# A layer norm split in two inside a streaming decode kernel, and an output written as 32 rows of 128

## The chip, the cores and the metric

The kernel runs on one core of one Trainium2 chip. The metric is device time in microseconds (us): the median of several executions. Where two kernels are compared, the ratio is the mean time of one kernel's fast runs over that of the other's fast runs of the same rounds on the same chip, so it is not quite the quotient of the medians quoted beside it. Kernels are compared only within the same rounds.

## The reference, cut to what matters

Eight tokens (batch 8, one position each) of width 512 go through attention, feed-forward, attention, feed-forward. Each part is preceded by a layer norm and added to its input. Both attentions read the same caches: 8 batches x 8 key heads x 8192 positions x 128, for K and for V.

```python
def _layernorm(x, axis=-1, eps=1e-5):
    m = jnp.mean(x, axis=axis, keepdims=True)
    v = jnp.var(x, axis=axis, keepdims=True)
    return (x - m) / jnp.sqrt(v + eps)

x = A_x
x = x + _A_ref(_layernorm(x), A_k_cache, A_v_cache, A_wq, A_wo)   # 32 query heads, 4 to a key head
x = x + _B_ref(_layernorm(x), B_w1, B_w2)                          # 512 -> 1792, silu, -> 512
x = x + _A_ref(_layernorm(x), A_k_cache, A_v_cache, A_wq, A_wo)
x = x + _B_ref(_layernorm(x), B_w1, B_w2)
return x
```

## The kernel before

The caches of one batch are used for the first and at once for the second attention of that token, so they are read from memory once. Where token b changes from its first to its second attention, a short serial chain has to run: end of attention (called x2 here), norm, feed-forward, norm, queries, scores. I call such a place a crossing; there are eight, about 135 us apart. In the views below, `kts` is a slot that holds loaded keys (a K load, 2 MB), `ring` the cells that hold values (a V load, 0.5 or 1 MB), `sc` the scores, `ot` the products with the values (V matmuls) and `qtb` the queries of the second attention; a slot or a cell can be loaded again when the work that reads it is over.

The program is built by a small planner. Every piece of work is a node with an engine, an assumed duration, a priority and a list of nodes that must be over; the planner simulates the engines and so fixes the order of the instructions on each of them. Each engine is given its instructions in that order; the traces below show it keep to it (at the third crossing of the changed kernel a cast whose matmuls had ended at 391.15 starts at 397.68, after the instruction ahead of it has waited 7.16 us). Resources (`res("misc")` is one bank of PSUM) are tracked by name, and a semaphore wait follows from who last wrote or read a name.

```python
def norm_nodes(tag, prio, b0, nb, deps):
    at = 40 if nb == 1 else 472
    nm, st, sq = (MI[:, at + 8 * k:at + 8 * k + nb] for k in range(3))      # columns of the bank "misc"
    # ... cut: stats() = 8 small matmuls (minus the mean, the mean), squares() = 6 more, scaled() on ACT
    def vari():
        op(dve, lambda: dve.tensor_scalar(var[:, 0:1], nm, st, sq, op0=ALU.mult, op1=ALU.add), ...)
    def root():
        op(pool, lambda: pool.tensor_tensor(rstd[:, 0:nb], var[:, 0:nb], expo[:, 0:nb], ALU.pow),   # GpSimd
           reads=[res("var"), res("expo")], writes=[res("rstd")])
    def apply():
        op(dve, lambda: dve.tensor_scalar(
            xn[:, b0, :], xs[:, b0, :], nm, rstd[:, 0:1], op0=ALU.add, op1=ALU.mult), ...)
    # ... cut
    v = plan.add(f"{tag}.var", "DVE", 0.3 if nb == 1 else 0.6, vari, prio, [a])
    r = plan.add(f"{tag}.root", "POOL", 0.65 if nb == 1 else 1.6, root, prio, [v])
    return plan.add(f"{tag}.xn", "DVE", 0.3, apply, prio, [r])
```

The queries of the second attention come in three pieces (head groups 0, 1, and 2 with 3). All pieces go through the same columns of the bank "misc", so the matmuls of a piece wait until the cast of the piece before has read its result:

```python
    for g0, g1 in ((0, 1), (1, 2), (2, 4)):
        # ...
        pr = prio + 2 * (g0 > 0)
        m = plan.add(f"{tag}.q{g0}", "PE", 0.5 * (g1 - g0), mul, pr, wq0_n + deps + last)
        last = [plan.add(f"{tag}.qc{g0}", "DVE", 0.17, lambda ...: query_copy(...), pr, [m])]
```

And the softmax needs a maximum over partitions:

```python
    n1 = plan.add(f"mx{u}", "DVE", 0.6, mx, pr - 1, sn + [...])        # maximum of a partition's scores
    n2 = plan.add(f"ma{u}", "POOL", 0.45, mall, pr, [n1])              # partition_all_reduce on GpSimd
    n3 = plan.add(f"own{u}", "DVE", 0.17, own_max, pr - 1, [n2])       # waits for it
    n4 = plan.add(f"exp{u}", "ACT", 0.42, exp, pr, [n3] + ...)
```

## Time and profile before

| kernel before | value | from |
|---|---|---|
| time | 1140.11 us (1139.96 to 1141.31, 3 runs) | executions |
| span of the profiled run | 1143.2 us | page |
| stream of the caches | from 3 to 1127 us, 408 GB/s | windows |
| after the stream | 16.2 us | windows |
| GpSimd busy | 116.9 us, 10% of the span | page |

The table is read like this: one resource, the transfers, is busy all the time (DMA share 1.01 while the stream runs); everything else counts only where it makes the transfers stop, and after they have ended. The lines for it are in the prediction below.

### The profile page before, as it was taken

The numbers are of one execution on the slowest core, as the hardware profiler recorded it, in microseconds if no ns is written. First come the engines' busy times: TensorE is split into PE (matmuls) and PEld (weight loads), VectorE is DVE, ScalarE is ACT, GpSimd is POOL, SyncE is SP. The second block draws the span as 40 slices with busy tenths as digits, with TensorE's granted clock in tenths as the row PEclk, the third lists the DMA queues.
The fourth block names the chain that finished last, engine by engine and source line by source line (L and its number), as shares of the span: only waits on it lengthen the run. The fifth ranks groups of instructions, "written<-read, shape, count | busy, mean of one in ns | idle before, by whom it ended". The sixth has DMA issues, their size and how long they took to land.

```text
span 1143.2 us, 32166 instructions
## 1 busy us (share of the span) xinstructions
PE 715.6 (63%) x13836; PEld 395.4 (35%) x13836; DVE 605.6 (53%) x1750; ACT 153.5 (13%) x509; POOL 116.9 (10%) x295
## 2 busy tenths in 40 slices
PE   2545566675565765657565676567566576565885
PEld 1322333343332433334233333334233243232554
DVE  5753556626565356634566345662656526673331
ACT  0010111112111211111111111111111112111110
POOL 1000011101110001100111001100111101110110
PEclk9665686657667677656667567765777757776675
DMA  9999999999999999999999999999999999999994
GB/s 368 421 418 399 366 409 420 408 383 408 424 419 406 404 416 422 423 400 413 404 408 422 373 413 417 422 414 397 405 414 420 388 409 421 419 423 404 364 408 181
DMA packets 78926, 458.76 MB, mean 401 GB/s; under 512 B 8112, under 2 KB 14016, under 8 KB 51136
## 3 DMA queue, kind: packets, MB, share of 16 engines
q1 hardware_dynamic: 78784, 456.70, 98.4%
q8 instruction: 109, 1.79, 0.6%
q14 instruction: 33, 0.27, 0.1%
HBM read 456.66 MB, written 0.01 MB: 399 GB/s over the span
## 4 chain that ended last, share of the span: by engine, by line
DMA 67%; PE 19%; DVE 6%; issue 5%; ACT 2%; SPq 1%; POOL 1%; POOLq 0%; DVEq 0%; ACTq 0%
DMA ring<-in_A_v_cache_dram 53%; DMA ring<-in_A_wo_dram 9%; PE sc L897 8%; PE ot L1023 7%; DVE kts L842 3%; DMA kts<-in_A_k_cache_dram 2%; DMA kts<-in_A_v_cache_dram 2%; DMA w<-in_B_w_dram 2%; PE misc L724 1%; PE yt L1097 1%; PE ex L1045 1%; ACT ring L755 1%; SPq L414 1%; PE sc L929 1%; DVE part L1037 1%
## 5 line engine op out<-in xcount | busy, mean ns | idle before, releaser
L1023 PE MATMUL ot<-ring,p 128*8 128x256 bf16 x3904 | 243.2, 375 | 186.2 <-DMA ring<-in_A_v_cache_dram 178.1
L842 DVE STREAM_TRANSPOSE kts<-kts 128x1024 uint32<-128x1024 uint32 x256 | 308.0, 1223 | 27.6 <-DMA kts<-in_A_k_cache_dram 27.2
L897 PE MATMUL sc<-kts,bd 128*32 128x256 bf16 x4096 | 283.0, 406 | 34.3 <-DVE kts L842 19.7
L1023 PEld LDWEIGHTS ot<-ring,p 128*8 128x8 bf16 x3904 | 86.6, 97 | 262.0 <-DMA ring<-in_A_v_cache_dram 222.5
L897 PEld LDWEIGHTS sc<-kts,bd 128*32 128x32 bf16 x4096 | 116.4, 117 | 108.5 <-DVE bd L880 25.8
L923 ACT ACTIVATE p<-sc,small 128x256 bf16<-128x256 f32 x128 | 60.7, 474 | 412.2 <-DVE small L918 258.1
L914 POOL PARTITION_ALL_REDUCE small<-small x128 | 47.6, 372 | 617.8 <-DVE small L910 526.1
L1037 DVE TENSOR_TENSOR part<-ot,p 128x256 bf16<-128x256 f32 x128 | 53.1, 415 | 105.6 <-ACT p L1033 69.3
L1033 ACT ACTIVATE p<-ot 128x256 bf16<-128x256 f32 x128 | 48.9, 382 | 419.5 <-PE ot L1023 415.6
L929 PE MATMUL sc<-p,ident 128*32 128x256 bf16 x512 | 43.0, 323 | 84.1 <-ACT p L923 83.4
L880 DVE TENSOR_TENSOR bd<-sc,mask 128x64 bf16<-128x64 f32 x128 | 27.7, 216 | 104.4 <-PE sc L897 99.0
L943 POOL PARTITION_ALL_REDUCE small<-small x128 | 55.2, 431 | 228.4 <-DVE small L939 228.4
L909 DVE TENSOR_REDUCE small<-sc 128x1 f32<-128x256 f32 x128 | 53.3, 416 | 34.5 <-PE sc L897 34.4
L936 DVE STREAM_TRANSPOSE p<-sc 128x256 bf16<-128x256 bf16 x128 | 56.7, 443 | 12.8 <-PE sc L929 11.1
L929 PEld LDWEIGHTS sc<-p,ident 128*32 128x32 bf16 x512 | 15.4, 109 | 112.1 <-ACT p L923 110.4
L1045 PE MATMUL ex<-diag,p 128*128 128x4 bf16 x256 | 25.9, 171 | 36.0 <-DVE part L1037 21.5
L1097 PE MATMUL yt<-z,ring 128*128 128x4 bf16 x1024 | 36.8, 166 | 16.0 <-DMA ring<-in_A_wo_dram 15.4
L1097 PEld LDWEIGHTS yt<-z,ring 128*128 128x128 bf16 x1024 | 31.4, 102 | 39.7 <-DMA ring<-in_A_wo_dram 27.3
L1045 PEld LDWEIGHTS ex<-diag,p 128*128 128x128 bf16 x256 | 16.6, 104 | 80.7 <-ACT p L1033 49.2
L939 DVE TENSOR_SCALAR small<-hm,small 128x4 f32<-128x4 f32 x128 | 27.0, 211 | 31.3 <-ACT p L923 31.1
L918 DVE SCALAR_TENSOR_TENSOR small<-small,hm 128x4 f32<-128x4 f32 x128 | 19.2, 150 | 41.1 <-POOL small L914 40.9
L1074 DVE TENSOR_TENSOR z<-ex,rc 128x16 bf16<-128x16 f32 x64 | 10.5, 163 | 50.4 <-PE ex L1067 50.3
(96 smaller groups left out, 536.1 us busy)
## 6 DMA issues: line engine op xcount, KB each, us to landing
ring<-in_A_v_cache_dram SPq DMA_DIRECT2D x146, 1024.0 KB, 12.5
kts<-in_A_k_cache_dram SPq DMA_DIRECT2D x64, 2048.0 KB, 12.0
ring<-in_A_v_cache_dram SPq DMA_DIRECT2D x196, 512.0 KB, 7.8
ring<-in_A_wo_dram SPq DMA_DIRECT2D x64, 512.0 KB, 11.7
ring<-in_A_wq_dram SPq DMA_DIRECT2D x20, 512.0 KB, 12.6
kts<-in_A_v_cache_dram SPq DMA_DIRECT2D x5, 2048.0 KB, 20.9
kts<-in_A_wo_dram SPq DMA_DIRECT2D x2, 2048.0 KB, 14.9
w<-in_B_w_dram SPq DMA_DIRECT2D x2, 1792.0 KB, 14.9
```

Of the source, the lines that this page charges most:

```text
L842: op(dve, lambda: dve.transpose(v, v), reads=[], writes=[res("kt", g)], add=(q > 0))
L897: steps.append(lambda t=t, y=y, w=w: pe.matmul(sc[32 * t:32 * t + 32, 0:256], w, kv[:, 2 * t + y, q], start=(q == 0 and y == 0), stop=(q = ...
L909: op(dve, lambda: dve.tensor_reduce(mxr[si], sv, AX.X, ALU.max), reads=[res(*scr)], writes=[res("mxr", si)])
L923: op(act, lambda: act.activation(pt[:, :], sv, ACT.Exp, bias=bias[si], scale=SM_SCALE, accum_out=rsum[si]), reads=[res(*scr), res("bias", ...
L929: steps = [lambda P=P: pe.matmul(sc[32 * P:32 * P + 32, 256:512], src[:, P], pt[:, :], start=True, stop=True) for P in range(4)]
L936: op(dve, lambda: dve.transpose(pt[:, :], src), reads=[res(*scr)], writes=[res("p", sm)])
L943: op(pool, lambda: pool.partition_all_reduce(ssa[si], ssm[si], 128, bass.bass_isa.ReduceOp.add), reads=[res("mxp", si)], writes=[res("mxa" ...
L1023: steps.append(lambda t=t, c=c, k=k: pe.matmul(ot[32 * t:32 * t + 2 * R, 0:2 * DH], pt[:, k:k + 2 * R], vt[:, c, t], start=(P == 0 and c = ...
L1033: op(act, lambda: act.activation(pt[:, :], ot[:, 0:2 * DH], ACT.Copy), reads=[res("ot", o)], writes=[res("p", sm)])
L1037: op(dve, lambda: dve.tensor_tensor(part[:, :], ot[:, 0:2 * DH], pt[:, :], ALU.subtract), reads=[res("ot", o), res("p", sm)], writes=[res( ...
L1045: steps.append(lambda k=k, src=src, y=y: pe.matmul(EX[:, 0:R], src[:, y * DH:y * DH + DH], diag[:, R * y:R * y + R], start=(k == 0 and y = ...
L1097: steps.append(lambda j=j, dt=dt: pe.matmul(YT[:, dt * R:(dt + 1) * R], w[:, j, dt * 128:(dt + 1) * 128], zt[:, R * j:R * j + R], start=(g ...
```

## The change

The intent is to take the root of the variance off the chain. In place of (x - mean) x root ahead of the matmuls, only x - mean goes on; the products are linear, so the root can scale later steps: the tanh and the residual in the feed-forward, and the own maximum and the exponential in the second attention. Constants (4 and 128) are folded into the variance so that one root also brings the 0.5 of the silu and the scale of the softmax. The later query pieces also get a lower priority, and the output leaves as 32 rows of 128 by one matmul in place of 8 rows of 512 by four. The core of the diff:

```diff
+    def center_nodes(tag, prio, b, c, root_out, root_res, deps):
+        bs = slice(b, b + 1)
+        nm = YT[:, 16:17]
+        st, sq, steps = squares_of(bs, 1, 40, c)          # columns of the bank "misc"
+        def center():
+            op(dve, lambda: dve.tensor_scalar(xn[:, b, :], xs[:, b, :], nm, None, op0=ALU.add),
+               reads=[res("xs"), res("yt")], writes=[res("xn")])
+        def squares():
+            mms(steps, reads=[res("cst"), res("xs"), res("xd")], writes=[res("misc")])
+        def vari():
+            op(dve, lambda: dve.tensor_scalar(var[:, 0:1], nm, st, sq, op0=ALU.mult, op1=ALU.add),
+               reads=[res("misc"), res("yt")], writes=[res("var")])
+        def root():
+            op(pool, lambda: pool.tensor_tensor(root_out, var[:, 0:1], expo[:, 0:1], ALU.pow),
+               reads=[res("var"), res("expo")], writes=[root_res])
+        ... (cut)
+        v = plan.add(f"{tag}.var", "DVE", 0.3, vari, prio, [a, xc])
+        return xc, plan.add(f"{tag}.root", "POOL", 0.65, root, prio, [v])
 ... (cut)
-            op(act, lambda: act.activation(th, hp, ACT.Tanh, scale=0.5),
+            op(act, lambda: act.activation(th, hp, ACT.Tanh, scale=half),        # half = rstd for one token
 ... (cut)
-            pr = prio + 2 * (g0 > 0)
+            pr = prio if g0 == 0 or nb > 1 else count[0] - 3.5
 ... (cut)
-                mxp[si], mxa[si], -SM_SCALE, hm[:, :], op0=ALU.mult, op1=ALU.mult, accum_out=bias[si]),
+                mxp[si], mxa[si], sm_scale, hmm[:, :], op0=ALU.mult, op1=ALU.mult, accum_out=bias[si]),
-            op(act, lambda: act.activation(pt[:, :], sv, ACT.Exp, bias=bias[si], scale=SM_SCALE, accum_out=rsum[si]),
+            op(act, lambda: act.activation(pt[:, :], sv, ACT.Exp, bias=bias[si], scale=sm_scale, accum_out=rsum[si]),
 ... (cut)
-            ready = norm_nodes(f"c{b}.ln2", prio, b, 1, [n])
+            ready, scale_n[0] = center_nodes(
+                f"c{b}.ln2", prio, b, 128, srs[:, b % 2:b % 2 + 1], res("srs", b % 2), [n])
 ... (cut)
-            MI[0:NB, kt * 128:(kt + 1) * 128], xs[:, :, kt], ident[:, :], start=True, stop=True)
-            for kt in range(KT)]
+            MI[0:NB * KT, 0:128], xs[:, :, :].rearrange("p b k -> p (b k)"), ident[:, :], start=True, stop=True)]
```

## The prediction

> **What bounds the kernel now.** I read the page first: busy tenths, then the DMA queues.
>
> ```profile
> DMA  9999999999999999999999999999999999999994
> GB/s 368 421 418 399 366 409 420 408 383 408 424 419 406 404 416 422 423 400 413 404 408 422 373 413 417 422 414 397 405 414 420 388 409 421 419 423 404 364 408 181
> q1 hardware_dynamic: 78784, 456.70, 98.4%
> ```
>
> The transfer engines are busy in every slice but the last; no compute engine is (PE 63%, DVE 53%). So the caches' stream is the bound and the layer norms are not, except where the stream starves or has ended. The view by windows splits the run (columns: us, busy time of PE, PEld, DVE, ACT, POOL, then PE clock, DMA share, GB/s):
>
> ```profile
> 3.00:1127.00 1124.00, 706.29 (x13614) 388.79 (x13618) 602.00 (x1737) 151.08 (x504) 114.61 (x280) 0.68 1.01 408
> 1127.00:1143.20 16.20, 9.27 (x230) 6.64 (x218) 2.93 (x10) 1.16 (x4) 0.55 (x1) 0.50 0.03 11
> ```
>
> The stream runs for 1124 us at 408 GB/s; then come 16 us of pure chain at half the PE clock. Windows of 2 us show where the stream sags. I counted the shortfall against 416 GB/s, about what the better slices hold: 21 us in all, 17.6 us of it around the eight places where a token passes from its first to its second attention (norm, feed-forward, norm, queries). About 1.2 us of each is a plain lower rate, with 17 to 19 V loads of 512 KB one by one instead of 1 MB pairs. Two places have a real gap that lies after the norms, the first and the last. The first:
>
> ```profile
> 122.00:124.00 2.00, 2.00 (x56) 1.62 (x56) 0.17 (x1) 0.00 (x0) 0.00 (x0) 0.50 0.49 193
> 124.00:126.00 2.00, 1.31 (x28) 0.62 (x20) 0.95 (x5) 0.00 (x0) 0.39 (x1) 0.50 0.39 84
> 126.00:128.00 2.00, 1.80 (x40) 0.87 (x33) 1.04 (x5) 0.56 (x2) 0.44 (x1) 0.76 0.80 319
> ```
>
> That is (223 + 332 + 97) x 2 / 416 = 3.1 us lost. The timeline there says why: the next K load needs a slot that is free only when the second attention has scored it, so it waits for norm, queries and scores:
>
> ```profile
> 117.77 0.16 DVE L599 SCALAR_TENSOR_TENSOR xs<-misc,xs 128x4 bf16<-128x4 f32 x1 [3.33 <-PE misc L592]
> 119.61 0.29 DVE L544 TENSOR_SCALAR xn<-xs,misc,rstd 128x4 bf16<-128x4 bf16 x1 [0.74 <-POOL rstd L539]
> 119.96 0.59 PE L724 MATMUL misc<-xn,wq 128*128 128x1 bf16 x16 [1.42 <-DVE xn L544]
> 122.01 1.01 PE L724 MATMUL misc<-xn,wq 128*128 128x1 bf16 x32
> 124.55 3.41 SPq L414 DMA_DIRECT2D kts<-in_A_k_cache_dram  x2
> ```
>
> The last place loses about 2.6 us between 1072 and 1082 (231, 311, 377, 305, 373 and 353 GB/s in six windows). And the end of the timeline, the last token's final norm and output:
>
> ```profile
> 1133.87 0.16 DVE L1167 TENSOR_TENSOR xs<-yt,xs 128x4 bf16<-128x4 f32 x1 [0.68 <-PE yt L1114]
> 1134.09 0.38 PE L504 MATMUL misc<-xs,cst 128*128 128x1 bf16 x8 [0.26 <-DVE xs L1167]
> 1134.45 0.19 PE L522 MATMUL misc<-cst 128*128 128x1 bf16 x2
> 1134.69 0.29 DVE L529 TENSOR_SCALAR var<-misc 128x1 f32<-128x1 f32 x1 [0.65 <-PE misc L522]
> 1135.05 0.55 POOL L539 TENSOR_TENSOR rstd<-var,expo 128x1 f32<-128x1 f32 x1 [24.29 <-DVE var L529]
> 1135.71 0.29 DVE L544 TENSOR_SCALAR xn<-xs,misc,rstd 128x4 bf16<-128x4 bf16 x1 [0.74 <-POOL rstd L539]
> 1136.06 1.66 PE L574 MATMUL misc<-xn,w 128*128 128x1 bf16 x56 [1.42 <-DVE xn L544]
> 1140.17 0.59 PE L1275 MATMUL misc<-ident,xs 128*8 128x128 bf16 x4 [0.25 <-DVE xs L599]
> 1140.81 0.68 DVE L1283 CAST ring<-misc 8x512 bf16<-8x512 f32 x1 [0.69 <-PE misc L1275]
> 1141.51 0.31 SPq L1297 DMA_DIRECT2D out_dram<-ring  x1
> ```
>
> From x done (1134.03) to the first up-projection matmul (1136.06) is 2.03 us: statistics, variance, root, apply, one after the other.
>
> [...] The trace has about 166 and 304 ns at clock 0.50[...] The cast of 512 takes 678 ns in the trace and one of 32 columns 193 ns, a slope of 1.01 ns[...] The new store writes 32 pieces of 256 B[...].
>
> **The change, part by part.**
> *Norm at the end.* The same 14 small matmuls and the same square and root remain, but only four matmuls and one add stand before the up-projection. Four matmuls: first at +0.06 us, 166 ns with three more at a pitch of 31 ns (eight take 0.38), 0.26. Hand-over 0.05. The add with one pointer operand: 0.22 (such 128x4 forms take 211 to 230 ns; the present one with two takes 289). Hand-over 0.06. Sum 0.65 us. The ten other matmuls, which the new program order also puts before the up-projection, end at 1134.64, 0.61 us after x, so they fit. Root: ready at about 1135.6, before up ends at about 1136.3. Gain 2.03 - 0.65 = 1.38. The tanh now has a scale pointer: -0.09.
> *Output.* One matmul of 128 columns in place of four: 0.59 to 0.30, gain 0.29. Cast 128 columns in place of 512: 0.68 - 384 x 1.01 ns = 0.29, gain 0.39. Store: 0, give or take 0.2. All of the end together: 1.38 - 0.09 + 0.29 + 0.39 = 2.0 us, all on the path.
> *First crossing.* Its first norm hides: the down-projection waits until 116.07 for w2 anyway. Its second norm takes 117.93 to 119.96, again 2.03, so 1.38 goes. The comparison of instruction order shows more: all 32 scores of the first slot now come before the last 32 query matmuls, which took 1.01 us ahead of the K load. The load leaves 2.4 us earlier; of a gap of 3.1 us I count 2.3.
> *Last crossing.* Two norms save 1.38 each. Today the second query start lies a further 1.5 us behind xn because 24 V matmuls stand in the queue between; the new order has none there. Queries start about 4 us earlier and V work is spread between the scores, so ring cells come free sooner. Of the 2.6 us I count 1.5.
> *Six crossings between.* The stream never stands still after their norms, so 4 us off the chain meets a wire that is occupied. The order shows 192 single and 148 paired V loads in place of 196 and 146; a pair seems to save 0.1 to 0.2 us, 0.3 in all. With small sags, 0.7.
> *Added and hidden.* 64 exps longer by about 0.09 us (ACT is 13% busy), one setup op, the second root beside the queries. Nothing on the path.
> Sum: 2.0 + 2.3 + 1.5 + 0.7 = 6.5 us. 1140.1 - 6.5 = 1133.6; I say 1133.8.
>
> **Rivals.** *All but the end is hidden:* the stream keeps its 1124 us, only 2.0 us go: 1138.1. For it: DMA share about 1.0 nearly everywhere. Against: the gap at 122 to 128 hangs visibly on the norm. *The new order gives it back:* the scheduler has moved every load after the first crossing, later query pieces have lower priority, and most middle crossings now have 21 single V loads in a row where there were 19; sags of 1.5 us just before a crossing (238 to 246, 648 to 654) come and go with such order. Two more of those: 1137 to 1141. *The crossings gain more:* if PE blocked on the norm holds ring cells, as PE is near full at half clock there (3.1 to 3.9 of 4 us between 372 and 392), each middle crossing could give another 0.5 us: 1130. *A new wait:* tanh or the exp waits for the root, or the 256 B store is slow; well under 1 us at the end.
>
> **Range and chances.** The end is sure to half a us; the two gaps may give 1.5 to 5; order noise is worth 2 to 3 us either way. 1129.5 to 1138.0 holds it 8 times in 10. 2% is 22.8 us, more than the whole shortfall of the stream: faster 0.01, within 0.985, slower 0.005.
>
> **What would show it.** Right: x done to up-projection 0.6 to 0.8 us at the end; output matmul 0.3, cast 0.28; first K load after the first crossing near 122.2; the low windows there nearly gone; stream over near 1122; about 14 us from its end to the last instruction. Wrong: the stream ends at 1127 as before (first rival), new sags at middle crossings (second), mean rate above 412 GB/s (third), or PE waiting for POOL after the up-projection.

The 166 and 304 ns in it are means of matmuls of one and of 128 columns in the kernel before (L1114 and L1275).

## The result, and the profile after

The changed kernel takes **1170.17 us** (1168.95 to 1171.63, 4 runs) against 1140.03 us (1138.99 to 1141.31, 4 runs) of the kernel before in the same rounds: ratio 1.0264, 95% interval [1.0246, 1.0282]. It is 30 us slower, far outside the predicted range.

The first view to look at is the same as before, the page's line of transfer rates in 40 slices:

```profile
GB/s 373 417 421 399 351 395 421 413 387 383 416 421 408 329 418 420 420 381 366 420 419 417 384 338 417 425 413 386 356 422 420 411 340 410 417 422 396 298 404 232
```

And the same split by windows (us, busy time of PE, PEld, DVE, ACT, POOL, PE clock, DMA share, GB/s):

```profile
3.00:1157.00 1154.00, 705.88 (x13654) 390.17 (x13654) 606.15 (x1740) 157.77 (x505) 115.34 (x283) 0.67 0.99 397
1157.00:1170.00 13.00, 7.14 (x187) 5.19 (x179) 2.02 (x9) 0.86 (x3) 0.55 (x1) 0.50 0.04 14
```

The stretch after the stream became shorter, 13.0 us for 16.2. The stream itself became 30 us longer at the same bytes, 1154 us at 397 GB/s for 1124 us at 408. So the whole loss lies in the stream, and the rates show where: from the middle of the first half on, every fifth slice or so sags, among them to 329, 338 and 340 GB/s, where the kernel before had 373 and more in its middle crossings (its line stands in the prediction). Those are the crossings. In windows of 44 us around each (from 14 us before x2 to 30 us after) I counted the shortfall against 416 GB/s, as the prediction does (its 17.6 us come from windows of its own): 4.5, 3.1, 1.6, 1.1, 3.1, 1.8, 1.5 and 4.3 us before, 20.9 us in all; 5.3, 3.0, 6.7, 6.0, 7.7, 6.6, 6.1 and 9.2 us after, 50.6 us in all. The difference, 29.7 us, is the loss. Nearly all of it lies in the last six crossings and not in the first, where I had looked.

So one crossing in the middle has to be read line by line. The third, in the timeline of the kernel before (start, duration, engine, line, operation, and in brackets the idle time before it and what ended that):

```profile
383.24 0.56 POOL L539 TENSOR_TENSOR rstd<-var,expo 128x1 f32<-128x1 f32 x1 [6.16 <-DVE var L529]
...
389.00 0.17 DVE L705 CAST qtb<-misc 128x8 bf16<-128x8 f32 x1 [1.34 <-PE misc L724]
390.54 0.33 SPq L414 DMA_DIRECT2D kts<-in_A_k_cache_dram  x1
390.95 0.23 DVE L910 TENSOR_SCALAR small<-hneg,small 128x4 f32<-128x4 f32 x1
392.38 0.38 POOL L914 PARTITION_ALL_REDUCE small<-small  x1 [8.59 <-DVE part L1037]
392.80 0.16 DVE L918 SCALAR_TENSOR_TENSOR small<-small,hm 128x4 f32<-128x4 f32 x1 [0.97 <-POOL small L914]
```

The same place in the changed kernel:

```profile
386.07 0.29 DVE L544 TENSOR_SCALAR var<-yt,misc 128x1 f32<-128x1 f32 x1 [0.68 <-PE misc L765]
386.43 0.55 POOL L548 TENSOR_TENSOR srs<-var,expo 128x1 f32<-128x1 f32 x1 [4.50 <-DVE qtb L746]
...
390.08 0.23 DVE L954 TENSOR_SCALAR small<-hneg,small 128x4 f32<-128x4 f32 x1
...
397.11 0.39 POOL L958 PARTITION_ALL_REDUCE small<-small  x1 [10.13 <-issue]
397.53 0.22 DVE L962 SCALAR_TENSOR_TENSOR small<-small,srs,hmm 128x4 f32<-128x4 f32 x1 [7.16 <-POOL small L958]
...
397.68 0.16 DVE L746 CAST qtb<-misc 128x4 bf16<-128x4 f32 x1
...
397.90 1.01 PE L765 MATMUL misc<-xn,wq 128*128 128x1 bf16 x32 [6.42 <-DVE qtb L746]
...
400.70 1.52 SPq L416 DMA_DIRECT2D kts<-in_A_k_cache_dram  x1
```

The reader is to see three things here.

1. In both kernels the first all-reduce (L914, L958) starts long after the power on the same engine has ended: 392.38 - 383.80 = 8.6 us before, 397.11 - 386.98 = 10.1 us after. In the changed kernel its input is ready at 390.31 (L954) and nothing else holds it: the bracket says "issue". In these 10.1 us GpSimd is busy with nothing; its queue holds only two records of 11 ns, shown further below.
2. Before, that time lay beside other work: the variance and the root came *first*, and norm, queries and scores followed, so that the input of the all-reduce was ready only at 391.18, 1.2 us before GpSimd was. After, the root comes *beside* the queries, and the input is ready 3.3 us after the root has ended; the chain waits 6.8 us.
3. The own maximum (L962) waits for the all-reduce at the head of the vector engine's queue, and the cast of the second query piece (L746 at 397.68) stands behind it, though its matmuls had ended at 391.15. The 32 matmuls of the last piece wait for that cast (6.42 us), and everything behind them on PE with them. Until 397.9 the transfers live on loads already issued; then they starve, as windows of 2 us show:

```profile
396.00:398.00 2.00, 0.10 (x4) 0.11 (x5) 0.31 (x3) 0.15 (x1) 0.39 (x1) 0.50 0.95 387
398.00:400.00 2.00, 1.79 (x48) 1.24 (x47) 1.29 (x6) 0.78 (x3) 0.44 (x1) 0.50 0.18 74
400.00:402.00 2.00, 2.00 (x40) 1.09 (x36) 0.22 (x1) 0.00 (x0) 0.00 (x0) 0.50 0.40 66
402.00:404.00 2.00, 2.00 (x40) 1.08 (x28) 0.38 (x2) 0.00 (x0) 0.00 (x0) 0.50 0.95 295
```

PE does next to nothing up to 398 (0.10 us in 2), and the wire pays for it from 398 to 404.

The second crossing limits this reading. Its all-reduce is as late (8.79 us after the power), the own maximum waits 6.24 us for it, and the cast stands behind; yet the shortfall is 3.0 us for 3.1. There the next K load had left at 251.67, 11.1 us after x2 and before the all-reduce (17.6 us after x2). In the six crossings that lost, it left 20.6 to 25.7 us after x2, behind the all-reduce; in the kernel before it left 14.5 to 18.8 us after x2 there. So a stall seems to cost most when the next loads stand behind it too. This is read from the traces; no experiment moved a K load alone.

What stands still on GpSimd? The gap from power to all-reduce is 5.9 us (before) and 6.1 us (after) at the first crossing and 8.2 to 10.2 us at the seven others of these two traces. The views by source line, which count GpSimd's queue (POOLq) too, hold records of one more kind. In the changed kernel at the third crossing:

```profile
L548 POOLq MODIFY_POOL_CONFIG  x2: 85/85/85, 369.5 to 369.5; - x2
L958 POOLq MODIFY_POOL_CONFIG  x2: 11/11/11, 387.2 to 387.2; - x2
```

The first pair comes right after the last all-reduce ahead of the crossing (it ended at 369.54) and has the line of the powers; the second comes right after the second power (386.98) and has the line of the all-reduce, which starts at 397.11. Over the whole run the all-reduce's line has 18 such records in both kernels, two of them in the gap at each crossing, of 11 ns each. What GpSimd does in the rest of the gap, no trace here shows. That the gap comes from the power ahead of the all-reduce, the experiments show: with an all-reduce in the power's place, the next one follows its input by 0.09 us at the third crossing.

The end of the timeline, for the parts of the prediction that lie there:

```profile
1161.38 0.16 DVE L1211 TENSOR_TENSOR xs<-yt,xs 128x4 bf16<-128x4 f32 x1 [0.68 <-PE yt L1158]
...
1162.27 1.65 PE L609 MATMUL misc<-xn,w 128*128 128x1 bf16 x56
1163.96 0.29 DVE L544 TENSOR_SCALAR var<-yt,misc 128x1 f32<-128x1 f32 x1 [1.75 <-PE misc L609]
...
1164.96 0.27 ACT L615 ACTIVATE th<-misc,rstd 128x14 f32<-128x14 f32 x1 [3.19 <-POOL rstd L548]
...
1167.47 0.29 PE L1320 MATMUL misc<-ident,xs 128*32 128x128 bf16 x1 [0.32 <-DVE xs L634]
1167.79 0.28 DVE L1327 CAST ring<-misc 32x128 bf16<-32x128 f32 x1 [0.38 <-PE misc L1320]
1168.10 0.35 SPq L1341 DMA_DIRECT2D out_dram<-ring  x1
```

From x done (1161.54) to the up-projection it is now 0.73 us. But the variance (L544) does not run beside the up-projection: it waits 1.75 us for it, "PE misc L609". Its sums lie in the bank "misc", which the up-projection writes too, at other columns; the kernel tracks the bank under one name, so the read waits for the last write of that name. The root follows late, and the tanh starts at 1164.96, 1.0 us after the up-projection has ended (1163.92).

### The profile page after: what moved, and what is told of

Read it like the earlier page. It is cut to its first block, busy times and chain, and to the rows that moved or that the text cites. A ratio compares the mean times of both kernels' runs of the same rounds, so it can differ in the third digit from the quotient of the medians.

```text
span 1169.9 us, 32157 instructions
## 1 busy us (share of the span) xinstructions
PE 713.0 (61%) x13833; PEld 395.4 (34%) x13833; DVE 608.9 (52%) x1751; ACT 159.9 (14%) x509; POOL 117.4 (10%) x301
## 5 line engine op out<-in xcount | busy, mean ns | idle before, releaser
L1067 PE MATMUL ot<-ring,p 128*8 128x256 bf16 x3904 | 237.9, 366 | 200.0 <-DMA ring<-in_A_v_cache_dram 190.7
L1067 PEld LDWEIGHTS ot<-ring,p 128*8 128x8 bf16 x3904 | 81.7, 95 | 262.8 <-DMA ring<-in_A_v_cache_dram 226.6
L941 PEld LDWEIGHTS sc<-kts,bd 128*32 128x32 bf16 x4096 | 119.7, 119 | 106.7 <-DVE bd L924 25.5
L958 POOL PARTITION_ALL_REDUCE small<-small x128 | 47.6, 372 | 641.2 <-DVE small L954 480.9
L967 ACT ACTIVATE p<-sc,small,srs 128x256 bf16<-128x256 f32 x64 | 36.1, 564 | 227.0 <-DVE qtb L746 63.5
L967 ACT ACTIVATE p<-sc,small 128x256 bf16<-128x256 f32 x64 | 30.4, 474 | 215.9 <-DVE small L962 189.8
L765 PE MATMUL misc<-xn,wq 128*128 128x1 bf16 (+1 forms) x576 | 19.5, 166 | 36.4 <-DVE qtb L746 28.0
## 6 DMA issues: line engine op xcount, KB each, us to landing
kts<-in_A_wo_dram SPq DMA_DIRECT2D x2, 2048.0 KB, 14.5
```

The source lines that it names most:

```text
L941: steps.append(lambda t=t, y=y, w=w: pe.matmul(sc[32 * t:32 * t + 32, 0:256], w, kv[:, 2 * t + y, q], start=(q == 0 and y == 0), stop=(q = ...
L958: op(pool, lambda: pool.partition_all_reduce(mxa[si], mxp[si], 128, bass.bass_isa.ReduceOp.max), reads=[res("mxp", si)], writes=[res("mxa" ...
L967: op(act, lambda: act.activation(pt[:, :], sv, ACT.Exp, bias=bias[si], scale=sm_scale, accum_out=rsum[si]), reads=[res(*scr), res("bias", ...
L1067: steps.append(lambda t=t, c=c, k=k: pe.matmul(ot[32 * t:32 * t + 2 * R, 0:2 * DH], pt[:, k:k + 2 * R], vt[:, c, t], start=(P == 0 and c = ...
```

## The experiments

Three theories stood at the start. **A**: the first all-reduce after a power comes late (5.9 to 10.2 us behind it at the crossings of the two kernels), and the queues behind it stand. **B**: the planner's new order of cache loads (single V loads in place of pairs, other slots) makes the sags. **C**: the low priority of the later query pieces makes them, by itself.

**No power ahead of the all-reduce, everything else equal.** The root becomes an all-reduce of the variance, so GpSimd has no power at the crossings. The result is wrong (relative error 0.030); the order of instructions on PE, DVE, ACT and of the transfers is identical to that of the changed kernel.

```diff
-            op(pool, lambda: pool.tensor_tensor(root_out, var[:, 0:1], expo[:, 0:1], ALU.pow),
+            op(pool, lambda: pool.partition_all_reduce(root_out, var[:, 0:1], 128, bass.bass_isa.ReduceOp.max),
```

> The changed kernel with one operation replaced: GpSimd's power, which makes the root of the variance for a single token, becomes an all-reduce of the same 128 values[...] (the result is wrong on purpose). Program order of TensorE and VectorE is the same, instruction for instruction. Theory A ([...]the first all-reduce of the second attention is now ready for it too early, and everything queued behind its user on VectorE and TensorE stands, V matmuls too, so the stream starves): the eight gaps vanish, 1133 to 1141 us. Theory B (the scheduler's new order of loads and its 21 single V loads in a row cost the time): no change, 1163 to 1173 us. Theory C (the lower priority of the later query pieces alone does it): no change either, above 1160 us.

Measured: 1138.51 us (1137.00 to 1142.83, 4 runs) against 1141.86 us (7 runs), ratio 0.997 [0.9931, 1.0009]. The third crossing in its timeline:

```profile
381.10 0.37 POOL L548 PARTITION_ALL_REDUCE srs<-var  x1 [4.52 <-DVE qtb L746]
384.79 0.23 DVE L954 TENSOR_SCALAR small<-hneg,small 128x4 f32<-128x4 f32 x1
385.11 0.38 POOL L958 PARTITION_ALL_REDUCE small<-small  x1 [3.64 <-DVE qab L1099]
385.52 0.22 DVE L962 SCALAR_TENSOR_TENSOR small<-small,srs,hmm 128x4 f32<-128x4 f32 x1 [0.44 <-POOL small L958]
```

The all-reduce follows its input by 0.09 us, and the whole 30 us are gone; the shortfall at the crossings is 18.2 us. B falls here, since the order of loads is the same, and so does C, since the priority is. What remains is how much of the loss is the late all-reduce alone and how much the queue behind it.

**The old priority in the changed kernel.**

```diff
-            pr = prio if g0 == 0 or nb > 1 else count[0] - 3.5
+            pr = prio + 2 * (g0 > 0)
```

> The changed kernel with the old priority of the later query pieces: their two casts stand on VectorE ahead of the instruction that waits for the first all-reduce again. Theory A: [...]only 1.6 us of query matmuls are moved in front of the wait: partly better, 1148 to 1163 us. Theory B: as slow as changed, above 1163. Theory C: all of it comes back, below 1145 us.

Measured: 1154.10 us (1151.73 to 1154.66), ratio 1.0098 [1.0071, 1.0125]. The all-reduce is still late, but the casts of all query pieces run ahead of it:

```profile
384.69 0.17 DVE L746 CAST qtb<-misc 128x8 bf16<-128x8 f32 x1 [1.34 <-PE misc L765]
386.63 0.23 DVE L954 TENSOR_SCALAR small<-hneg,small 128x4 f32<-128x4 f32 x1
389.41 0.39 POOL L958 PARTITION_ALL_REDUCE small<-small  x1 [6.50 <-issue]
389.83 0.22 DVE L962 SCALAR_TENSOR_TENSOR small<-small,srs,hmm 128x4 f32<-128x4 f32 x1 [2.33 <-POOL small L958]
```

Of the 2.6% that the change cost, 1.7% go with the priority. The shortfall is 35.5 us.

**The low priority alone, in the kernel before.** The edit is the reverse of the one above.

> The kernel before with nothing changed but the priority of the later query pieces. Theory A: the root still stands in the chain[...]; the first all-reduce waits 1 to 2 us longer and one cast is behind it: 1139 to 1150 us. Theory B: nothing, 1137 to 1143. Theory C: most of the loss appears, above 1158 us.

Measured: 1140.47 us (1138.57 to 1142.28), ratio 0.9982 [0.9955, 1.0009]. The priority by itself costs nothing. It costs only together with something.

**The planner is told of the gap.** The changed kernel, with one empty node that keeps GpSimd occupied for 9 us after the second root in the plan. No instruction is added; only the order changes.

```diff
-        return xc, plan.add(f"{tag}.root", "POOL", 0.65, root, prio, [v])
+        r = plan.add(f"{tag}.root", "POOL", 0.65, root, prio, [v])
+        if c == 128:
+            plan.add(f"{tag}.library", "POOL", 9.0, lambda: None, prio - 1, [r])
+        return xc, r
```

> The changed kernel, but the scheduler is told that GpSimd is occupied for 9 us after the root of the second norm (an empty entry, no instruction): it orders the other engines' work so that what needs no all-reduce goes first. Theory A: the stall goes[...], 1134 to 1145 us, VectorE's casts ahead of the first wait and the gaps of the stream mostly gone. Theory B: a different order of loads, so anything, but with no reason to be under 1155. Theory C: the priority is unchanged, so above 1160 us.

Measured: 1141.56 us (1141.10 to 1141.99), ratio 0.9992 [0.9967, 1.0016]. This is the most instructive run, since the gap is still there:

```profile
388.85 0.17 DVE L749 CAST qtb<-misc 128x8 bf16<-128x8 f32 x1
...
389.61 0.73 SPq L416 DMA_DIRECT2D kts<-in_A_k_cache_dram  x1
389.77 1.10 PE L944 MATMUL sc<-kts,bd 128*32 128x256 bf16 x16
...
390.90 1.10 PE L944 MATMUL sc<-kts,bd 128*32 128x256 bf16 x16
...
393.60 0.38 POOL L961 PARTITION_ALL_REDUCE small<-small  x1 [9.83 <-issue]
394.02 0.22 DVE L965 SCALAR_TENSOR_TENSOR small<-small,srs,hmm 128x4 f32<-128x4 f32 x1 [4.30 <-POOL small L961]
```

The vector engine still waits 4.30 us for the all-reduce, but now nothing that others need stands behind it: the casts are done and the next 32 score matmuls (L944) and the next K load run inside the gap. A stall of this kind, behind the same power, costs 30 us in one order and nothing in another.

**The kernel before without a power.** The control for the first experiment: all roots of single tokens by an all-reduce. Its output is wrong, which doesn't matter for the time.

```diff
+            if nb == 1:
+                op(pool, lambda: pool.partition_all_reduce(rstd[:, 0:1], var[:, 0:1], 128, bass.bass_isa.ReduceOp.max),
+                   reads=[res("var"), res("expo")], writes=[res("rstd")])
```

> The kernel before with its single-token roots as an all-reduce too (wrong result on purpose)[...]. Theory A[...]: the first all-reduce comes 1 to 2 us earlier at each crossing and the stream gains little, 1136 to 1141 us. [...]

Measured: 1140.83 us (1136.78 to 1145.49, 6 runs) against 1140.69 us (11 runs), ratio 1.0002 [0.9983, 1.0022]. The kernel before pays nothing for the gap that it also has.

**The kernel before with a later gap.** Six powers that nobody needs, after the second norm's root, push the gap back by 3.7 us; the norm is not split.

```diff
+            if "ln2" in tag:
+                for _ in range(6):
+                    op(pool, lambda: pool.tensor_tensor(rstd[:, 1:2], var[:, 0:1], expo[:, 0:1], ALU.pow),
+                       reads=[res("var"), res("expo")], writes=[res("spare")])
```

> The kernel before with six needless powers of 128 values on GpSimd after the root of each second norm. The norm itself does not wait for them[...]. Theory A: [...]the kernel before becomes as slow as changed, 1150 to 1172 us, with the same gaps in the stream. Theories B and C: order of loads and priorities are those of before, so 1138 to 1144 us.

Measured: 1154.46 us (1151.20 to 1159.63, 4 runs), ratio 1.0113 [1.0092, 1.0135].

```profile
384.00 0.55 POOL L539 TENSOR_TENSOR rstd<-var,expo 128x1 f32<-128x1 f32 x1 [6.16 <-DVE var L529]
384.52 3.68 POOL L543 TENSOR_TENSOR rstd<-var,expo 128x1 f32<-128x1 f32 x6
...
391.03 0.23 DVE L914 TENSOR_SCALAR small<-hneg,small 128x4 f32<-128x4 f32 x1
395.77 0.38 POOL L918 PARTITION_ALL_REDUCE small<-small  x1 [7.58 <-issue]
```

The input of the all-reduce (L914) is ready as early as in the kernel before; the chain waited 1.2 us there (391.18 to 392.38) and waits 4.5 us here (391.26 to 395.77). 3.7 us more at eight places on an engine that is 10% busy cost 13 us of 1141. That is in the range expected, but at its low end: the kernel does not become as slow as the changed one. The split norm does the same from the other side: there the gap stays, and the work that covered it moves away.

**Sums in their own bank, and the plan told of the gap.** The false wait at the variance is taken away by putting the sums into free columns of the bank of the mean; the planner's empty node stays.

```diff
-        st, sq, steps = squares_of(bs, 1, 40, c)
+        st, sq, steps = squares_of(bs, 1, 17, c, YT)
-            mms(steps, reads=[res("cst"), res("xs"), res("xd")], writes=[res("misc")])
+            mms(steps, reads=[res("cst"), res("xs"), res("xd")], writes=[res("yt")], add=True)
-               reads=[res("misc"), res("yt")], writes=[res("var")])
+               reads=[res("yt")], writes=[res("var")])
```

> The changed kernel[...] as in the run before, and in addition the sums for the variance in columns of the bank of the mean instead of the bank that the up-projection and the query matmuls write. In the changed kernel the variance waits for that next matmul group (1.75 us behind it at the end), which puts the root 1 us behind the up-projection and delays tanh. Theory: about 1 us comes back at the end and the root is early at each crossing[...]: 1136 to 1141 us, tanh within 0.1 us of the last up-projection matmul. If the wait of the variance were harmless: the same as without it, 1141 to 1142.

Measured: 1139.31 us (1136.44 to 1143.50, 6 runs) against 1140.69 us, ratio 0.9992 [0.9975, 1.001]. Nothing that the interval can tell from the kernel before. The false wait at the end is gone: the tanh starts at 1131.28, 0.04 us after the up-projection has ended (1131.24).

**The root on the vector engine.** Same columns, no power on GpSimd at the crossings, and a correct result: a first guess by integer shift and subtraction and two Newton steps, eight small instructions of the vector engine. In the trace they take 1.6 us at the end of the kernel and lie beside the up-projection.

```diff
-            op(pool, lambda: pool.tensor_tensor(root_out, var[:, 0:1], expo[:, 0:1], ALU.pow), ...)
+            op(dve, lambda: dve.tensor_scalar(t.bitcast(U32), v.bitcast(U32), 1, None, op0=ALU.logical_shift_right), ...)
+            op(dve, lambda: dve.tensor_scalar(y.bitcast(U32), t.bitcast(U32), -1.0, float(0x5f375a86), op0=ALU.mult, op1=ALU.add), ...)
+            for k in range(2):
+                op(dve, lambda: dve.scalar_tensor_tensor(t, y, v, y, op0=ALU.mult, op1=ALU.mult), ...)
+                op(dve, lambda: dve.tensor_scalar(t, t, -0.5, 1.5, op0=ALU.mult, op1=ALU.add), ...)
+                op(dve, lambda dst=dst: dve.tensor_tensor(dst, y, t, ALU.mult), ...)
-        return xc, plan.add(f"{tag}.root", "POOL", 0.65, root, prio, [v])
+        return xc, plan.add(f"{tag}.root", "DVE", 1.5, root, prio + 0.5, [v])
```

> The changed kernel, correct, with the single-token roots on VectorE by shift, subtraction and two Newton steps (eight small operations), and the sums of the variance in the bank of the mean. [...] Theory A: no gap at the crossings, so what I predicted for the change appears, less what eight operations cost VectorE: 1133 to 1139 us, below the kernel before. Theory B: the order of loads is much as in the changed kernel, above 1155 us.

Measured: 1136.64 us (1135.64 to 1139.30, 6 runs) against 1140.69 us, ratio 0.9972 [0.9958, 0.9985]. This version beats both kernels. The third crossing:

```profile
386.70 0.23 DVE L966 TENSOR_SCALAR small<-hneg,small 128x4 f32<-128x4 f32 x1
387.02 0.37 POOL L970 PARTITION_ALL_REDUCE small<-small  x1 [21.20 <-DVE qab L1111]
387.42 0.22 DVE L974 SCALAR_TENSOR_TENSOR small<-small,srs,hmm 128x4 f32<-128x4 f32 x1 [0.43 <-POOL small L970]
```

The shortfall at the crossings is 16.5 us, 4.4 less than before, and the way from x done to the issue of the output at the end is 1133.34 - 1127.14 = 6.20 us, 1.3 less than before (7.48).

**Late gap and low priority together, in the kernel before.** If the priority is what doubles the cost of a late all-reduce, it should do so here too.

> The kernel before, with six needless powers on the GpSimd engine after the second norm's root[...] and with the low priority of the later query pieces, together; the norm isn't split. Alone the first cost about 13 us and the second nothing. [...]the two together cost more than their sum: 1160 to 1172 us. If what costs in the changed kernel is something else of the split norm (its scale on the exponentials, its shared bank), the two together cost their sum: 1150 to 1156 us.

Measured: 1157.10 us (1152.88 to 1162.12, 4 runs) against 1142.70 us (11 runs), ratio 1.0131 [1.0094, 1.0167]. My range is missed; next to the late gap alone (1.0113) nothing that the intervals can separate was added. The trace says what is different. Where PE waits for a query cast, in the changed kernel:

```profile
PE misc L765 <- DVE qtb L746: 28.0, 5, 6.8
```

(us in all, times, longest; the cast stands behind the waiting maximum at seven of the eight crossings.) The view of waits of this experiment has no such line. In the plan of the kernel before, the low priority leaves the second piece's cast ahead of the maximum that waits; in that of the changed kernel it lands behind. So it is not the priority as such, but the place of that one cast.

**The second query piece early, in the changed kernel.** Only groups 2 and 3 keep the low priority.

```diff
-            pr = prio if g0 == 0 or nb > 1 else count[0] - 3.5
+            pr = prio + 2 * (g0 > 0) if g0 < 2 or nb > 1 else count[0] - 3.5
```

> The changed kernel with the old priority for the second query piece alone; the third and fourth keep the low one. The run of the kernel before[...] missed my range (1157 instead of 1160 to 1172), and its trace has no wait of the query matmuls for a cast, which the changed kernel has five times, 28 us in all: there the second piece's cast stands on the vector engine behind the maximum that waits for the reduction. This edit puts the second piece's matmuls and cast ahead of it[...]. If that blocked cast is what made 1170 out of 1154, this gives 1151 to 1158 us (ratio 1.010 to 1.016) and no such wait in the trace. If the low priority costs in another way, 1163 to 1172.

Measured: 1157.58 us (1154.48 to 1164.57, 6 runs) against 1142.77 us (11 runs), ratio 1.0144 [1.0115, 1.0174]; so the gap to the kernel before falls from 30 us to 15, and the median and the ratio lie in the range expected.

```profile
385.93 0.16 DVE L746 CAST qtb<-misc 128x4 bf16<-128x4 f32 x1 [0.20 <-PE misc L765]
...
390.00 0.95 PE L765 MATMUL misc<-xn,wq 128*128 128x1 bf16 x32
393.02 0.39 POOL L958 PARTITION_ALL_REDUCE small<-small  x1 [7.34 <-issue]
```

The cast is done before the scores, the matmuls of the last piece run inside the gap, and the wait of the query matmuls for a cast is gone. The edit reshuffles other instructions too, so 15 us is what this order saves, not the price of one cast.

**The root on the vector engine, with the old priority.**

> The changed kernel with the root on the vector engine and the sums in columns of their own (the version that beat both kernels), and with the old priority of the later query pieces. [...]it is the same as that version: 1134 to 1139 us, within 0.4%. If the priority costs by itself wherever the norm is split, this is faster by 5 us or more.

Measured: 1143.72 us (1140.02 to 1144.90, 6 runs) against 1142.70 us (11 runs, 1138.97 to 1147.00) on another chip, ratio 1.0012 [0.9986, 1.0038]. The median is above my range; the kernel before was slower on this chip as well (1142.70 us for 1140.69). By the ratios, 0.9972 and 1.0012, the two versions are 0.4% apart, with intervals that do not quite touch. Not faster by 5 us, so the low priority is not a cost by itself in a split norm; whether it is a small gain, this does not settle.

**The output part alone, in the kernel before.**

> The kernel before with one part of the change alone: the output leaves as 32 rows of 128 by one matmul and one cast. The prediction gave it 0.7 us at the very end (matmul 0.59 to 0.30, cast 0.68 to 0.29 us) and nothing elsewhere: 1139.4 us, ratio 0.9994; in the profile the stretch from x done to the issue of the output transfer falls from 7.48 to about 6.8 us. A ratio of 1.01 or more would mean that the output part carries a share of the loss.

Measured: 1141.10 us (1138.46 to 1144.86, 6 runs) against 1142.70 us, ratio 0.9991 [0.9963, 1.0018]: within the noise, so the time can't confirm 0.7 us. The profile can: from x done (1134.58) to the issue of the output (1141.35) it is 6.77 us, for 7.48 before, with the matmul at 0.29 and the cast at 0.28 us. The output part has no share in the loss.

The ratios side by side:

| gap on GpSimd | second query piece | run | ratio |
|---|---|---|---|
| none | behind the waiting maximum | changed, root as all-reduce | 0.997 |
| beside other work | ahead | kernel before, low priority | 0.998 |
| covered by the plan | ahead | changed, plan told of the gap | 0.999 |
| late | ahead | changed, old priority | 1.010 |
| late | ahead | kernel before, six powers | 1.011 |
| late | ahead | kernel before, six powers, low priority | 1.013 |
| late | ahead | changed, second piece early | 1.014 |
| late | behind the waiting maximum | changed | 1.026 |

The four other runs have no late gap (the two with the root on the vector engine, the plan told of the gap with the sums moved, the kernel before without a power); they lie between 0.997 and 1.001.

One experiment was not made: keeping the sums in the bank "misc" and giving only their columns a name of their own. The vector engine would then read the bank while PE writes to it with no order between them; whether that is safe, and what it would save, was not shown.

## Why the prediction was wrong

**The step that failed** is what the prediction says under "Added and hidden": "64 exps longer by about 0.09 us (ACT is 13% busy), one setup op, the second root beside the queries. Nothing on the path." The root itself is hidden, 0.55 us. What follows it on GpSimd is not: the first all-reduce afterwards comes 6 to 10 us later. The trace of the kernel before showed this, 8.6 us from L539 to L914 at the third crossing, and I had read it as an engine that had nothing to do. I gave GpSimd the cost of its instructions and not that of the gap between them. The root was placed first in the chain, and this order hid the gap; the change removed exactly that cover. The sizes: 1.0 to 1.4% (11 to 16 us) for the late all-reduce, as the four runs with it and a well-placed cast show, and the rest of the 2.6% for the order that put the cast of the second query piece behind the waiting maximum. This division is an estimate from the ratios, since each of these edits moved other instructions too.

**The rivals.** "A new wait" was the right heading with the wrong place and size: the exponential does wait, but not for the root, and not "well under 1 us". "The new order gives it back" named the lower priority of later query pieces, with which 1.2 to 1.7 of the 2.6% go (the second piece early, the old priority); its other reason (single V loads) was wrong, since the same order without the power takes 1138.5 us. The two sags that it quotes come to 1.8 us each by its own measure, not 1.5.

**The six crossings between.** The prediction has 0.7 us of gain there. They lost 4.6 to 5.1 us each by the shortfalls above, except the second, which lost nothing (3.1 and 3.0). Against the run with the root as all-reduce, whose order is the same, the second lost too, 3.0 us for 1.2.

**The first crossing.** The K load leaves at 122.15, where the prediction had 122.2 (124.55 before). But the 2.3 us were not won: the all-reduce came at 126.02, 6.10 us after the power, and the shortfall is 5.3 us for 4.5. Without the power it is 2.9 (root as all-reduce, K load at 122.64) and 4.1 us (root on the vector engine, K load at 123.61), 1.6 and 0.4 less than before. So part of the gain is there once the power is gone, but less than the 2.3 us counted on.

**The last crossing.** 1.5 us were expected; its shortfall went from 4.3 to 9.2 us. In the two versions free of the power it is 5.4 (root as all-reduce) and 4.1 us (root on the vector engine). So the gain did not come even there; why not, I have not tested. One reading was off: the second queries started 1.1 us behind xn in the kernel before (1065.01 to 1066.10), not 1.5.

**The end.** x done to up-projection: 0.73 us, predicted 0.65. Output matmul 0.29 (0.30), cast 0.28 (0.29): right. The store was to cost nothing more, give or take 0.2 us: from its issue to the end of the span it is 1.7 us before (1141.51 to 1143.2) and 1.8 us after (1168.10 to 1169.9). "Root: ready at about 1135.6, before up ends at about 1136.3" failed: the wait through the bank "misc" put the root after the up-projection and took 1.0 us back. The end gained 7.48 - 6.56 = 0.92 us instead of 2.0. The prediction asked for "PE waiting for POOL after the up-projection" as a sign of error; it was ACT that waited. With the sums in the other bank it gained 1.5 (root on GpSimd) and 1.3 (root on the vector engine). In both, x done to up-projection is 1.12 us in place of 0.73: the other bank has one name too, and the subtraction of the mean now waits for all the sums.

**The exponentials.** The added pointer costs 564 - 474 = 90 ns, in the page's group lines of the changed kernel:

```profile
L967 ACT ACTIVATE p<-sc,small,srs 128x256 bf16<-128x256 f32 x64 | 36.1, 564 | 227.0 <-DVE qtb L746 63.5
L967 ACT ACTIVATE p<-sc,small 128x256 bf16<-128x256 f32 x64 | 30.4, 474 | 215.9 <-DVE small L962 189.8
```

The tanh with its scale pointer takes 273 ns (L615) where it took 183 without (L580), again 90 ns. The prediction has 0.09 us for each; no trace had shown it before this run.

**The range.** It was built from errors of terms in the sum. The loss came from a term that was not in it.

## What to carry to other kernels

Before moving an instruction to another place in an engine's queue, look in the trace at the idle time *behind* it: an engine that has time to spare may be hiding a cost there, which shows only once its cover is moved. With in-order queues, the cost of a late result is set by what stands behind the instruction that waits for it; here gaps of 6 to 10 us on GpSimd cost nothing or 30 us by order alone. A planner has to be told of such a gap, or the engine that causes it has to be kept out: here the root on another engine was best.

## What the runs leave open

- At all eight crossings of both kernels the all-reduce that follows a power comes late, each time with two MODIFY_POOL_CONFIG records in the gap. What sets the length of the gap is open: it is 5.9 and 6.1 us at the first crossing of the two kernels and 8.2 to 10.2 us at the others; at the third crossing 6.50 us with the old priority, 7.34 with the second piece early, 7.58 with six more powers and 9.83 with the plan told of the gap. These kernels ran on different chips.
- In the other direction, from all-reduce to power, there is a gap as well: after the last crossing of the changed kernel, in the norm of the seven other tokens, the power starts 7.54 us after the all-reduce has ended (1129.02 to 1136.56), 1.8 us after its input (1134.77). At the crossings of the two kernels it does not show, since the first power comes 9.7 to 14.5 us after the last all-reduce.
